# An attention of three stages ahead of two MLPs: four-head loads of q and k, and batch 0's normalisation moved between engines

## The chip, the cores and the metric

One core of a Trainium2 chip runs the whole program in one launch. The metric is the device time of an execution in microseconds (us), the median of several. The engines are TensorE (PE), VectorE (DVE), ScalarE (ACT), GpSimd (POOL) and the queues that issue DMAs, here those of SyncE (SP) and of ACT.

## The reference

```python
def _attn_ref(q, k, v):                 # B, H, S, D = 4, 8, 576, 64;  m = 32
    q_lm = q.reshape(B, H, m, S // m, D).mean(axis=3)      # 18 rows per landmark
    k_lm = k.reshape(B, H, m, S // m, D).mean(axis=3)
    A, Bm, C = sm(q, k_lm), sm(q_lm, k_lm), sm(q_lm, k)    # softmax of scale * a @ b.T
    Z = Bm.T / (norm1(Bm) * norminf(Bm) + 1e-6)
    for _ in range(6):
        Z = 2 * Z - Z @ Bm @ Z
    return A @ Z @ C @ v
def _moe_ref(x, w_gate, w_val, w_out, rms_g):              # 2304 x 512, d_ff = 1536
    xn = x / sqrt(mean(x * x) + 1e-6) * rms_g
    g = xn @ w_gate
    return (g * sigmoid(g) * (xn @ w_val)) @ w_out
def _moe2_ref(x, w_in, w_out, s, b):                       # 2304 x 512, d_ff = 2048
    r = maximum(x @ w_in, 0)
    return (s * r * r + b) @ w_out
```

The attention's output, heads side by side, is x of the first MLP, whose output is x of the second. The weights come as 64-bit floats.

## The kernel before

The program computes the attention batch by batch. For batch 0 it does so alone; the attention of batch b + 1 is laid under the first MLP's products of batch b. A batch has 12 units, one for each 128 columns of w_gate and w_val. A unit forms a small product of the two weight tiles with the attention's last factor (`gw`; the U product, L993, in `fused`), splits it into a high and a low part (`uh`, `ul`, L1001 to L1004), and then multiplies both with the high and low parts of A (`xh`, `xl`) in three products each (L1016, in `first_mm`), once for each half of the batch (hf). L1032 to L1038 form the hidden value from the results, and L1061 or L1065 multiply it with w_out. The second MLP follows (L975, L1091).

Attention, with its lines: q and k are loaded by `load_heads` (L446), for each of them in two groups g of four heads. A group fills a tile of 128 partitions, 32 for each head, each partition holding the 18 rows of one landmark. In batches 0 and 1 (`fine` is false) the heads of group g are 2h + g, so the load takes one DMA for each head. L474 sums the 18 rows (batch 0: on DVE; batch 1: by POOL, in the steps L488 to L493), L498 transposes the sums, L528 with L532 (ACT) transposes q and k themselves. L660 are scores: of C (`c_side`: maximum L677, Exp L687, transposed back L704 and evicted L714, times v in L726) and of A (`a_side`: transposed L756, maximum L757, subtracted L758, Exp L759, summed L762, scaled L767, transposed L768). L556 to L593 form Bm, L586 with L631 are the steps of the iteration for Z. L790 (DVE) opens the last part, the normalisation: L828 forms x, L834 (ACT) its squares, L848 sums them over columns, L855 to L859 make the root's reciprocal, L861 spreads it to a diagonal, L866 multiplies it out to all partitions, L872 scales A with it, and L876 (ACT) and L878 (POOL or DVE) split A into `xh` and `xl`. Only then can the batch's products run.

Weights of the first MLP are converted once, in batch 0 (`narrow`): a DMA (L906, L904) fills one of three `stage` tiles, ACT does L917 and L919, DVE L921 and L924. The result is also stored to DRAM (`kept`) and read back for the other batches.

The order of the work is made by a planner in the program (`Scheduler`). Each operation is given with the engines it may run on, an assumed duration on each, and a key; the planner plays the program with these durations and at each step gives an engine the ready operation with the smallest key. `S_.by_path` sets the keys of an attention batch by the longest path behind each operation. What the planner writes is fixed: each engine executes its own list in order. While PE would stand idle by the plan in the first 60 us of plan time, `warm` (L1248) puts filler products into its list, one for each 0.1 us.

## Time and profile before

| | us |
|---|---|
| median of 3 runs | 906.83 |
| lowest, highest | 901.38, 908.39 |
| the profiled execution, its own time | 903.9 |
| span of its instructions | 902.2 |
| PE busy in it | 870.2 (96%) |
| DVE busy | 700.9 (78%) |
| ACT busy | 430.0 (48%) |
| POOL busy | 114.4 (13%) |

The span runs from the first to the last instruction that the profiler has recorded. The mean granted clock of PE is 0.987 of full speed. Busy shares are means over stages of different kinds; the filler products count as busy too.

### The profile page before, as it was taken

How to read it: one execution, taken by the hardware profiler on the slowest of the kernel's cores; microseconds unless marked ns; L12 is line 12 of the kernel's file. 1: busy time of each engine (PE TensorE's matmuls, PEld its weight loads, DVE VectorE, ACT ScalarE, POOL GpSimd, SP SyncE). 2: the span in 40 equal slices, each digit the busy share in tenths (PEclk: the TensorE clock that was granted, in tenths of full speed). 3: DMA queues.
4: the chain of work that ended last, by engine and by line, in shares of the span. 5: the costliest groups of instructions: out<-in, count | busy, mean ns of one | idle time of the engine just before them, and what ended most of it. 6: DMA issues, size and time to landing. Idle time of an engine off the chain costs nothing.

```text
span 902.2 us, 17055 instructions
## 1 busy us (share of the span) xinstructions
PE 870.2 (96%) x6453; PEld 726.4 (81%) x6453; DVE 700.9 (78%) x1486; ACT 430.0 (48%) x902; POOL 114.4 (13%) x152
## 2 busy tenths in 40 slices
PE   8897899899999999999999999999999999999997
PEld 5576666798788898899888988888888888888896
DVE  5768889889888889799889866676667666666686
ACT  3565566535465345555656533343343334333453
POOL 0442034500465004300000000000000000000000
PEclk9898999999999999999999999999999999999999
DMA  7778998886444432348887200010001000100100
GB/s 162 198 214 283 247 280 236 271 241 216 119 144 141 143 116 84 106 146 272 286 262 252 56 1 1 0 47 1 1 1 47 1 1 1 47 1 1 27 22 24
DMA packets 72899, 105.99 MB, mean 117 GB/s; under 512 B 25968, under 2 KB 46448, under 8 KB 72816
## 3 DMA queue, kind: packets, MB, share of 16 engines
q1 hardware_dynamic: 72240, 103.45, 38.3%
q10 hardware_dynamic: 576, 1.44, 0.7%
q8 instruction: 51, 0.84, 0.4%
q14 instruction: 32, 0.26, 0.1%
HBM read 90.70 MB, written 14.16 MB: 116 GB/s over the span
## 4 chain that ended last, share of the span: by engine, by line
PE 83%; DVE 8%; DMA 5%; ACT 2%; issue 1%; SPq 1%; ACTq 0%; DVEq 0%
PE bank L975 22%; PE bank L1091 22%; PE bank L1016 15%; PE bank L1065 12%; PE bank L1061 3%; PE bank L993 3%; DMA region<-in_q_dram 2%; DVE cmag L921 2%; DMA stage<-in_moe_w_out_dram 2%; PE bank L648 1%; PE bank L828 1%; DMA stage<-in_moe_w_gate_dram 1%; PE bank L1248 1%; DVE wl L893 1%; DVE rawg L924 1%
## 5 line engine op out<-in xcount | busy, mean ns | idle before, releaser
L1016 PE MATMUL bank<-xh,uh 128*128 128x288 f32 x384 | 124.2, 323 | 6.4 <-DVE hbuf L1034 3.1
L975 PE MATMUL bank<-xh,ul 128*128 128x512 f32 (+1 forms) x320 | 117.7, 368 | 0.0
L975 PE MATMUL bank<-xh,uh 128*128 128x512 f32 (+1 forms) x320 | 117.6, 368 | 0.0
L975 PE MATMUL bank<-xl,uh 128*128 128x512 f32 (+1 forms) x320 | 117.6, 368 | 0.0
L1016 PE MATMUL bank<-xl,uh 128*128 128x288 f32 x384 | 114.8, 299 | 0.0
L1016 PE MATMUL bank<-xh,ul 128*128 128x288 f32 x384 | 114.7, 299 | 0.0
L1091 PE MATMUL bank<-wh,hh 128*128 128x512 f32 x288 | 112.4, 390 | 0.3 <-DVE hh L892 0.3
L1091 PE MATMUL bank<-wl,hh 128*128 128x512 f32 x288 | 112.3, 390 | 0.0
L1226 ACT ACTIVATE hbuf<-bank 128x512 f32<-128x512 f32 (+1 forms) x79 | 43.9, 556 | 143.4 <-PE bank L975 143.3
L1091 PE MATMUL bank<-wh,hl 128*128 128x512 f32 x288 | 112.0, 389 | 0.0
L1016 PEld LDWEIGHTS bank<-xh,uh 128*128 128x128 f32 x384 | 73.6, 192 | 27.3 <-issue 5.0
L1065 PE MATMUL bank<-hh,wh 128*128 128x288 f32 x288 | 87.9, 305 | 1.1 <-ACT xbuf L1075 1.1
L1065 PE MATMUL bank<-hl,wh 128*128 128x288 f32 x288 | 84.9, 295 | 0.1
L1065 PE MATMUL bank<-hh,wl 128*128 128x288 f32 x288 | 84.6, 294 | 0.0
L893 DVE TENSOR_TENSOR hl<-hbuf,hh 128x512 fp32r<-128x512 f32 (+2 forms) x123 | 73.1, 595 | 2.3
L1016 PEld LDWEIGHTS bank<-xl,uh 128*128 128x128 f32 x384 | 73.7, 192 | 0.5
L1016 PEld LDWEIGHTS bank<-xh,ul 128*128 128x128 f32 x384 | 73.7, 192 | 0.0
L975 PEld LDWEIGHTS bank<-xh,uh 128*128 128x128 f32 x320 | 60.2, 188 | 11.1
L975 PEld LDWEIGHTS bank<-xl,uh 128*128 128x128 f32 x320 | 60.0, 188 | 10.9
L975 PEld LDWEIGHTS bank<-xh,ul 128*128 128x128 f32 x320 | 60.1, 188 | 10.2
L917 ACT ACTIVATE ca<-stage 128x512 f32<-128x512 f32 x68 | 45.9, 675 | 42.6 <-DMA stage<-in_moe_w_out_dram 12.0
L892 DVE CAST uh<-region 128x512 fp32r<-128x512 f32 x56 | 23.9, 426 | 54.4 <-PE bank L975 54.4
(193 smaller groups left out, 1822.9 us busy)
## 6 DMA issues: line engine op xcount, KB each, us to landing
rawo<-kepto SPq DMA_DIRECT2D x84, 256.0 KB, 3.3
rawg<-keptg SPq DMA_DIRECT2D x36, 512.0 KB, 3.9
stage<-in_moe_w_out_dram SPq DMA_DIRECT2D x28, 512.0 KB, 5.2
stage<-in_moe_w_in_dram SPq DMA_DIRECT2D x16, 512.0 KB, 4.6
stage<-in_moe_w_gate_dram SPq DMA_DIRECT2D x12, 512.0 KB, 5.3
stage<-in_moe_w_val_dram SPq DMA_DIRECT2D x12, 512.0 KB, 5.5
keptg<-rawg SPq DMA_DIRECT2D x12, 512.0 KB, 6.3
region<-in_k_dram SPq DMA_DIRECT2D x32, 144.0 KB, 5.3
```

Source lines behind the costliest of these rows:

```text
L648: nc.tensor.matmul(out=ps.t[:, 0:HC], lhsT=part(u, "bd")[:, 128 * e:128 * e + 128], rhs=part(y, "t").rearrange("p (t e i) -> p t e i", e=2 ...
L892: else e.tensor_copy(out=hi(), in_=src())), r=r, w=[wh], pair=True)
L893: b = op({"dve": t_dve(n), "pool": t_pool(n)}, key, lambda e: e.tensor_tensor(out=lo(), in0=src(), in1=hi().bitcast(F32), op=ALU.subtract) ...
L917: op(("act", 0.08 + t_act(512)), key, lambda e: e.activation(out=a.t, in_=word(1).bitcast(F32), func=ACTF.Copy, scale=2.0 ** -112), r=[st, ...
L921: op(("dve", t_dve(512)), key, lambda e: e.scalar_tensor_tensor(out=m.t, in0=word(1), scalar=-2 ** 31, in1=m.t, op0=ALU.bitwise_and, op1=A ...
L975: nc.tensor.matmul(out=ps.t[:, 0:n], lhsT=w[a].t[:, ks], rhs=x[y].t[:, kd, 0:n], start=(kd == 0 and i == 0), stop=(kd == KD - 1 and i == 2))
L993: nc.tensor.matmul(out=pU[g].t[m, 0:256], lhsT=gw[b].t[p, m], rhs=r.t[p, :, 128 * k:128 * k + 128], start=True, stop=True)
L1016: nc.tensor.matmul(out=ps.t[:, 0:HC], lhsT=u[a].t[:, 256 * g + 128 * part:256 * g + 128 * part + 128], rhs=x[y].t.rearrange("p k n -> p (k ...
L1061: nc.tensor.matmul(out=A[c].t[:, 0:HC], lhsT=r.t[:, 128 * c:128 * c + 128], rhs=h.t, start=(f == 0), stop=(f == F1 - 1))
L1065: nc.tensor.matmul(out=A[c].t[:, 0:HC], lhsT=w[a].t[:, 128 * c:128 * c + 128], rhs=hs[y].t[:, 0:HC], start=(f == 0 and i == 0), stop=(f == ...
L1091: nc.tensor.matmul(out=A[c].t, lhsT=hs[a].t[:, s], rhs=w[y].t, start=(f == 0 and i == 0), stop=(f == F2 - 1 and i == 2))
L1226: e.activation(out=r.t[:, 0:n], in_=ps.t[:, 0:n], func=ACTF.Relu) if e is nc.scalar
```

## The change

In batches 0 and 1 group g now holds heads 4g to 4g + 3, which lie behind each other in DRAM, so one DMA loads all 128 partitions; q of batch 0 goes on SP's queue as well, and the planner's assumed duration of such a load is 3.64 in place of 5.2. What follows needs heads 2h + g, so scores, and the product for Bm, take each head from the tile that holds it (`loaded`), read both tiles, and both tiles of k (or q) are transposed ahead of the first of them. In batch 0 the four squares are added up on DVE before L848, which then has one product in place of four for each third (until now only the other batches did so); the diagonal (L861) and the low parts of A (L878) are given to DVE alone instead of to DVE or POOL. A Tanh on a dummy tile loads ACT's table behind the second root. The U product of batch 0's first unit has a smaller key. In every batch the diagonal, the adds and the low parts are marked as sharing the planner's port between DVE and POOL (`pair`).

```diff
@@ -417,6 +417,9 @@
         def dp(n):
             return {"dve": t_dve(n), "pool": t_pool(n)}
 
+        def near(n):
+            return {"dve": t_dve(n)} if first else dp(n)
+
         pair = xs[1, b] = (Buf(x_r[0]), Buf(x_r[1]))
         area = {"t": (0, SEG * D), "bd": (SEG * D, 256)}
 
@@ -442,13 +445,17 @@
                 t = src[nm, g] = Buf(qk_r[nm, g])
 
                 def load_heads(e, t=t, a=a, g=g):
+                    if not fine:
+                        e.dma_start(
+                            out=t.t.rearrange("p (t d) -> p t d", d=D),
+                            in_=a[b, 4 * g:4 * g + 4].rearrange("h (i t) d -> (h i) t d", t=SEG))
+                        return
                     for h in range(4):
                         e.dma_start(
                             out=t.t[32 * h:32 * h + 32].rearrange("p (t d) -> p t d", d=D),
                             in_=a[b, 2 * h + g].rearrange("(i t) d -> i t d", t=SEG))
 
-                at(("act" if first and nm == "q" else "sp", 2.2 if first and nm == "q" else 5.2),
-                   -0.3 if b else 0, load_heads, w=[t])
+                at(("sp", 5.2 if fine else 3.64), -0.3 if b else 0, load_heads, w=[t])
...
+        def loaded(g, h):
+            n = 2 * h + g
+            return n // 4, slice(32 * (n % 4), 32 * (n % 4) + 32)
 
         lmT, bd, tt = {}, {}, {}
...
@@ -552,10 +565,10 @@
             for g in range(2):
                 if not fine:
                     for h in range(4):
-                        p = slice(32 * h, 32 * h + 32)
+                        i, p = loaded(g, h)
                         nc.tensor.matmul(
-                            out=pB.t[p, 32 * g:32 * g + 32], lhsT=bd["q", g].t[0:D, p],
-                            rhs=bd["k", g].t[0:D, p], start=True, stop=True)
+                            out=pB.t[32 * h:32 * h + 32, 32 * g:32 * g + 32], lhsT=bd["q", i].t[0:D, p],
+                            rhs=bd["k", i].t[0:D, p], start=True, stop=True)
                     continue
                 for e in range(2):
                     nc.tensor.matmul(
@@ -640,7 +653,7 @@
                     else e.tensor_copy(out=zy(1), in_=v2(pY2))), r=[pY2], w=[ZY])
 
         def scores(ps, nm, g, hf, p0, r, w):
-            d, t = bd["kq"[nm == "k"], g], tt[nm, g]
+            other = "kq"[nm == "k"]
...
@@ -655,19 +668,21 @@
                 return
             def mm(_):
                 for h in range(4):
-                    p = slice(32 * h, 32 * h + 32)
+                    i, p = loaded(g, h)
                     e = slice(D * hf, D * hf + D)
                     nc.tensor.matmul(
-                        out=ps.t[p, 0:HC], lhsT=d.t[e, p],
-                        rhs=t.t[e].rearrange("p (t m) -> p t m", m=128)[:, :, p], start=True, stop=True)
-
-            at(("pe", SCORE), p0 + 0.02, mm, r=[d, *[(t, i) for i in range(3)], *r], w=[ps, *w])
+                        out=ps.t[32 * h:32 * h + 32, 0:HC], lhsT=bd[other, i].t[e, p],
+                        rhs=tt[nm, i].t[e].rearrange("p (t m) -> p t m", m=128)[:, :, p], start=True, stop=True)
+
+            at(("pe", SCORE), p0 + 0.02, mm, r=[*[bd[other, j] for j in range(2)],
+                *[(tt[nm, j], i) for j in range(2) for i in range(3)], *r], w=[ps, *w])
 
 
         Cv = Buf(cv_r)
 
         def c_side(g, p0):
-            transposed("k", g, p0)
+            for j in (g,) if fine else (0, 1) if g == 0 else ():
+                transposed("k", j, p0)
...
@@ -739,7 +754,8 @@
 
         def a_side(hf, g, p0):
             if hf == 0:
-                transposed("q", g, p0)
+                for j in (g,) if fine else (0, 1) if g == 0 else ():
+                    transposed("q", j, p0)
...
@@ -834,13 +850,12 @@
                 at(("act", t_act(HC)), p0 + 0.01, lambda e, c=c, pX=pX, xq=xq: e.activation(
                     out=xq.t[:, HC * c:HC * c + HC], in_=pX.t[:, 0:HC], func=ACTF.Square), r=[pX], w=[(xq, c)])
             pS, pR, rs, dg = Buf(ps_r), Buf(ps_r), Buf(sm_r), Buf(a_ring)
-            if not first:
-                for c, n in ((2, 2 * HC), (1, HC)):
-                    at(dp(n), p0 + 0.03, lambda e, c=c, n=n, xq=xq: e.tensor_tensor(
-                        out=xq.t[:, 0:n], in0=xq.t[:, 0:n], in1=xq.t[:, HC * c:HC * c + n], op=ALU.add),
-                        r=[(xq, i) for i in range(KD)] if n > HC else [(xq, 0), (xq, c)],
-                        w=[(xq, 0)] + ([(xq, 1)] if n > HC else []))
-            n_sum = KD if first else 1
+            for c, n in ((2, 2 * HC), (1, HC)):
+                at(near(n), p0 + 0.03, lambda e, c=c, n=n, xq=xq: e.tensor_tensor(
+                    out=xq.t[:, 0:n], in0=xq.t[:, 0:n], in1=xq.t[:, HC * c:HC * c + n], op=ALU.add),
+                    r=[(xq, i) for i in range(KD)] if n > HC else [(xq, 0), (xq, c)],
+                    w=[(xq, 0)] + ([(xq, 1)] if n > HC else []), pair=True)
+            n_sum = 1
 
...
@@ -857,12 +872,15 @@
 
             at(("dve", 0.3), p0 + 0.06, s_rec, r=[pS], w=[rs])
             at(("act", 0.2 if first else 1.4), p0 + 0.07, lambda e, rs=rs: e.activation(
-                out=rs.t[0:NP, 0:3], in_=rs.t[0:NP, 0:3], func=ACTF.Sqrt), r=[rs, "table"], w=[rs])
-            at(dp(HC), p0 + 0.07, lambda e, rs=rs, dg=dg: e.tensor_tensor(
+                out=rs.t[0:NP, 0:3], in_=rs.t[0:NP, 0:3], func=ACTF.Sqrt), r=[rs, "table"], w=[rs, ("root", b, hf)])
+            if first and hf:
+                at(("act", 1.4), 0.0, lambda e: e.activation(out=spare, in_=spare, func=ACTF.Tanh),
+                   r=[("root", 0, 0), ("root", 0, 1)], w=["spare"])
+            at(near(HC), p0 + 0.07, lambda e, rs=rs, dg=dg: e.tensor_tensor(
                 out=dg.t[0:NP].rearrange("p (j c) -> p j c", j=3),
                 in0=ident[0:NP, 0:NP].unsqueeze(1).to_broadcast([NP, 3, NP]),
                 in1=rs.t[0:NP, 0:3].rearrange("p (j o) -> p j o", o=1).to_broadcast([NP, 3, NP]),
-                op=ALU.mult), r=[rs, "ident"], w=[dg])
+                op=ALU.mult), r=[rs, "ident"], w=[dg], pair=True)
...
@@ -875,9 +893,9 @@
                 at({"act": t_act(HC), "dve": t_dve2(HC)}, p0 + 0.09, lambda e, a=a, cols=cols: (
                     e.activation(out=part(0, "t")[:, cols], in_=a.t[:, 0:HC], func=ACTF.Copy) if e is nc.scalar
                     else e.tensor_copy(out=part(0, "t")[:, cols], in_=a.t[:, 0:HC])), r=[a], w=wh, pair=True)
-                at(dp(HC), p0 + 0.1, lambda e, a=a, cols=cols: e.tensor_tensor(
+                at(near(HC), p0 + 0.1, lambda e, a=a, cols=cols: e.tensor_tensor(
                     out=part(1, "t")[:, cols], in0=a.t[:, 0:HC], in1=part(0, "t")[:, cols].bitcast(F32),
-                    op=ALU.subtract), r=[a, wh[0]], w=wl)
+                    op=ALU.subtract), r=[a, wh[0]], w=wl, pair=True)
...
@@ -994,7 +1012,7 @@
                         out=pU[g].t[m, 0:256], lhsT=gw[b].t[p, m],
                         rhs=r.t[p, :, 128 * k:128 * k + 128], start=True, stop=True)
 
-        op(("pe", U_PE), key, mm, r=[gw[b], (r, 0), (r, 1)], w=[*pU, (uh, "taken"), (ul, "taken")])
+        op(("pe", U_PE), key - 12 if not (b or f) else key, mm, r=[gw[b], (r, 0), (r, 1)], w=[*pU, (uh, "taken"), (ul, "taken")])
         for g in range(2):
             c = slice(256 * g, 256 * g + 256)
             op({"act": t_act(256), "dve": t_dve(256)}, key, lambda e, g=g, c=c: (
```

The lists that the planner makes of it differ on all engines. In the new program's lines, L449 is the four-head load, L924 the load of a weight part (L906 before), L955 the store L937.

SP's queue from its beginning, before; `stage` tiles are those of the weights:

```order
L446 DMA region<-in_k_dram 32x1152 x8
L460 DMA region<-in_v_dram 32x8x64 x18
L906 DMA stage_91<-in_moe_w_gate_dram 128x4x128
L446 DMA region<-in_k_dram 32x1152 x8
L446 DMA region<-in_q_dram 32x1152 x8
L906 DMA stage_91<-in_moe_w_val_dram 128x4x128
L937 DMA keptg_114<-rawg_85 128x1024
L460 DMA region<-in_v_dram 32x8x64 x18
L906 DMA stage_91<-in_moe_w_gate_dram 128x4x128
```

and now:

```order
L449 DMA region<-in_k_dram 128x1152 x2
L449 DMA region<-in_q_dram 128x1152 x2
L467 DMA region<-in_v_dram 32x8x64 x18
L924 DMA stage_91<-in_moe_w_gate_dram 128x4x128
L449 DMA region<-in_k_dram 128x1152 x2
L449 DMA region<-in_q_dram 128x1152 x2
L467 DMA region<-in_v_dram 32x8x64 x18
L924 DMA stage_91<-in_moe_w_val_dram 128x4x128
L955 DMA keptg_114<-rawg_85 128x1024
L454 DMA region<-in_k_dram 32x1152 x4
L924 DMA stage_91<-in_moe_w_gate_dram 128x4x128
```

(Of each run of three stage loads the first is shown; three small loads stand behind the first run in both.) The second group of v, batch 1's, now stands ahead of the fourth to sixth stage loads instead of behind them, and half of batch 2's k ahead of the seventh.

DVE's list in the last part of batch 0's attention, from L790 on, before (three pieces: its start, the parts of the fourth weight, the scaling of A):

```order
L790 TENSOR_TENSOR region<-bank_63,mask_74 128x128 x2
L798 TENSOR_TENSOR region<-region,mask_75 128x256
L855 TENSOR_SCALAR region<-bank_65 96x3
L810 TENSOR_TENSOR gw_106<-bank_64,gT 128x128
L921 SCALAR_TENSOR_TENSOR cmag_97<-stage_91,cmag_97 128x512
L924 SCALAR_TENSOR_TENSOR rawg_86<-ca_95,cmag_97 128x512
L872 TENSOR_TENSOR region<-region,bank_66 128x288 x2
L872 TENSOR_TENSOR region<-region,bank_63 128x288 x2
L1034 SCALAR_TENSOR_TENSOR hbuf<-hbuf,bank_70 128x288
```

and now, where L854 are the adds of squares, L879 the diagonal, L890 the scaling, L896 the low parts, L939 and L942 the weight conversion:

```order
L806 TENSOR_TENSOR region<-bank_67,mask_74 128x128 x2
L814 TENSOR_TENSOR region<-region,mask_75 128x256
L854 TENSOR_TENSOR region<-region 128x576
L854 TENSOR_TENSOR region<-region 128x288
L870 TENSOR_SCALAR region<-bank_68 96x3
L879 TENSOR_TENSOR xbuf<-ident,region 96x288
L890 TENSOR_TENSOR region<-region,bank_63 128x288 x2
L896 TENSOR_TENSOR xl_83<-region,xh_81 128x288 x2
L895 CAST xh_81<-region 128x288
L939 SCALAR_TENSOR_TENSOR cmag_97<-stage_91,cmag_97 128x512
L942 SCALAR_TENSOR_TENSOR rawg_86<-ca_95,cmag_97 128x512
L896 TENSOR_TENSOR xl_83<-region,xh_81 128x288 x2
```

The conversion of the fourth to sixth weight part has moved from between the normalisation's steps to behind the first low parts, and steps that POOL did stand in DVE's list.

PE's list where batch 1's attention ends and its first unit begins, before (L866 is the scaling product, L993 with `gw1` the U product of batch 1's first unit, L1061 products with w_out):

```order
L1061 MATMUL bank0_63<-hbuf_108,rawo2_90 128x288
L866 MATMUL bank6_69<-region_113,ones_72 128x288 x2
L993 MATMUL bank5_68<-rawg2_87,gw0_106 32x256
L1016 MATMUL bank4_67<-xh0_81,uh0_98 128x288
L1061 MATMUL bank2_65<-hbuf_108,rawo0_88 128x288
L1061 MATMUL bank2_65<-hbuf_108,rawo1_89 128x288
L993 MATMUL bank4_67<-rawg0_85,gw1_107 32x256
```

and now (L1011 is the U product, L884 the scaling product, L1079 the product with w_out, L1034 with `xh1` batch 1's first product):

```order
L1011 MATMUL bank6_69<-rawg0_85,gw1_107 32x256
L1079 MATMUL bank2_65<-hbuf_108,rawo0_88 128x288
L863 MATMUL bank7_70<-ones_72,region_113 96x1 x3
L1079 MATMUL bank1_64<-hbuf_108,rawo1_89 128x288
L884 MATMUL bank7_70<-region_113,ones_72 128x288
L884 MATMUL bank6_69<-region_113,ones_72 128x288
L1079 MATMUL bank0_63<-hbuf_108,rawo2_90 128x288
L1034 MATMUL bank4_67<-xh1_82,uh0_98 128x288
```

(Rows between are left out.) The scaling products of batch 1 now stand behind the U product of its first unit and close ahead of its first product; before they stood one unit further ahead.

## Rows read from the trace of the kernel before

**Rows 1.** Table of stretches: busy us (instructions) of each engine, clock, DMA share, GB/s

```profile
0.00:61.00 61.00, 52.44 (x627) 38.06 (x628) 38.57 (x110) 29.56 (x75) 14.64 (x24) 0.89 0.76 181
61.00:175.00 114.00, 100.49 (x967) 74.62 (x966) 99.52 (x225) 69.84 (x152) 40.20 (x52) 0.96 0.88 268
175.00:484.00 309.00, 303.73 (x2894) 265.69 (x2892) 269.97 (x622) 161.62 (x375) 59.56 (x77) 1.00 0.57 179
```

**Rows 2.** Timeline, first 30 us: start, duration, engine, line, what; in brackets idle before

```profile
0.80 8.41 ACTq L446 DMA_DIRECT2D region<-in_q_dram  x8
0.80 8.12 SPq L446 DMA_DIRECT2D region<-in_k_dram  x8
...
8.71 2.12 DVE L474 TENSOR_REDUCE region<-region 128x64 f32<-128x1152 f32 x1 [7.13 <-DMA region<-in_k_dram]
...
13.62 6.30 DVE L474 TENSOR_REDUCE region<-region 128x64 f32<-128x1152 f32 x3 [2.78 <-DMA region<-in_k_dram]
```

**Rows 3.** DMA rates in 40 slices: 2.5 to 13.5 (q, k), then 24.5 to 28 (weights first)

```profile
GB/s 369 369 268 201 184 235 201 184 201 218 268 268 201 184 201 218 184 201 201 218 268 268 201 184 201 218 201 184 201 218 268 268 201 184 201 218 141 139 174 203
DMA packets 1278, 2.40 MB, mean 218 GB/s; under 512 B 786, under 2 KB 786, under 8 KB 1278
...
GB/s 398 374 386 374 374 375 375 339 363 363 363 351 386 363 351 363 351 363 363 386 374 328 271 225 168 98 127 167 207 101 206 206 258 182 223 54 265 159 317 212
```

**Rows 4.** Timeline, 20 to 33 us: the first weight tile and who waits

```profile
20.64 0.45 SPq L906 DMA_DIRECT2D stage<-in_moe_w_gate_dram  x1
...
25.15 0.66 ACT L917 ACTIVATE ca<-stage 128x512 f32<-128x512 f32 x1 [2.57 <-DMA stage<-in_moe_w_gate_dram]
...
26.68 1.53 PE L726 MATMUL bank<-region 128*32 128x64 f32 x40 [2.20 <-ACT region L714]
...
32.03 1.21 PE L726 MATMUL bank<-region 128*32 128x64 f32 x40
...
32.23 0.29 DVE L631 SCALAR_TENSOR_TENSOR region<-region,bank 128x128 f32<-128x128 f32 x1 [4.33 <-issue]
```

**Rows 5.** Timeline, 43 to 61 us: the normalisation of batch 0 up to the first product

```profile
43.25 0.47 DVE L790 TENSOR_TENSOR region<-bank,mask 128x128 f32<-128x128 f32 x2
...
45.72 4.26 PE L848 MATMUL bank<-ones,xbuf 128*96 128x1 f32 x48
...
52.84 4.16 PE L1248 MATMUL bank<-ones 128*128 128x256 bf16 x35
...
58.53 1.54 POOL L878 TENSOR_TENSOR xl<-region,xh 128x288 fp32r<-128x288 f32 x2 [7.10 <-ACT xh L876]
...
59.45 1.58 PE L1248 MATMUL bank<-ones 128*128 128x256 bf16 x13
...
60.79 0.38 PE L1016 MATMUL bank<-xh,uh 128*128 128x288 f32 x1
```

**Rows 6.** Groups by line and form, first 80 us: busy us, mean ns, idle before

```profile
L872 DVE TENSOR_TENSOR region<-region,bank 128x288 f32<-128x288 f32 x4 | 1.6, 451 | 2.4 <-PE bank L866 2.4
```

**Rows 7.** Timeline, POOL and DVE: one instruction beside POOL's, and without

```profile
39.37 1.41 POOL L488 TENSOR_TENSOR region<-region 128x576 f32<-128x576 f32 x1
39.98 1.35 DVE L921 SCALAR_TENSOR_TENSOR cmag<-stage,cmag 128x512 int32<-128x512 int32 x1
...
76.91 0.68 DVE L921 SCALAR_TENSOR_TENSOR cmag<-stage,cmag 128x512 int32<-128x512 int32 x1
```

**Rows 8.** SP's queue: its waits up to 175 us (total, times, longest), then timeline

```profile
SPq L906 <- DVE cmag L921: 33.8, 14, 5.7
...
47.64 11.07 SPq L460 DMA_DIRECT2D region<-in_v_dram  x18
58.81 0.40 SPq L906 DMA_DIRECT2D stage<-in_moe_w_gate_dram  x1
```

**Rows 9.** Timeline: first hidden value of batch 0, last L866 and first product of batch 1

```profile
62.70 0.46 DVE L1034 SCALAR_TENSOR_TENSOR hbuf<-hbuf,bank 128x288 f32<-128x288 f32 x1 [2.23 <-ACT hbuf L1032]
...
161.00 0.72 PE L866 MATMUL bank<-region,ones 96*128 96x288 f32 x2 [2.69 <-DVE region L872]
...
175.07 0.51 PE L1016 MATMUL bank<-xh,uh 128*128 128x288 f32 x1
```

## The prediction

> **What bounds the kernel now.** I read the table of stretches first, then the timeline of the start, then the waits. From 175 us on, TensorE (PE) is busy 303.7 of 309 us at full clock, and this change leaves the order of PE's work the same from the sixteenth U product (L993) on, so that part can only be shifted, not shortened [rows 1]. What can shrink lies before. Up to 61 us the core computes batch 0's attention, on which every product waits; PE shows 52 busy us there, but much of it is filler. From 61 to 175 us nothing is full: PE 100.5 of 114 us, VectorE (DVE) 99.5, DMA engines at 0.88 [rows 1].
>
> In the start the reader is to see three things. First, k and q come in as 32-partition pieces, eight issues on each of two queues; the first segment sum starts at 8.71 us, the other three wait until 13.62 and end at 19.92 [rows 2]. Second, DVE stands still for 4.33 us before the first step of the inverse (L631): ScalarE (ACT) has waited 2.57 us for the first weight tile with the evictions queued behind it, PE's next group then waited for those evictions, and L631 for PE [rows 4]. Third, from the L790 that opens the last part (43.25 us) to the first product (L1016, 60.79) is 17.5 us, in which PE runs 63 filler products in three groups (35, 15 and 13) [rows 5]; its queue is in order, so real work stands behind them.
>
> **The sum** is made against the profiled execution, 903.9 us (span 902.2 and 1.7 around it), which is 2.9 under the median of the three runs.
>
> *Loads.* Sixteen 144 KB issues become four of 576 KB, all on SP; the ACT queue is freed of eight issues. In 32-partition form the engines were occupied throughout and moved 218 GB/s, while 128-partition weight tiles ran at some 365 GB/s [rows 3]. A 512 KB tile landed 4.5 us after its issue (20.64 to 25.15) [rows 4]; so I put k's first tile at 0.8 + 4.5 + 0.2 = 5.5 us and the next three 1.6 us apart (590 KB at 365 GB/s): 7.1, 8.7, 10.3. The four sums take 2.1 us each on DVE (6.30 / 3) [rows 2] and then run back to back, 5.5 to 13.9 instead of to 19.9: **−6.0**. Bounds: if the rate stays at 218 GB/s (2.7 us each, first at 6.6) they end at 16.8, −3.1; if only the bytes counted, the first landed at 2.4 and they ended at 10.8, −9. I take the weight tiles' rate since the new transfers have their 128 partitions.
> A rule of the Trainium skill speaks against this: "DMA: Bandwidth & Descriptors", in the section on why a DMA increments its semaphore by 16, says that a transfer is split over the largest number up to 16 that divides its slowest dimension, so 32 and 128 partitions both use 16 engines and the new form would have no more of them than the old. By that alone this term would be the −3.1 and the sum 897; the two rates in rows 3 say otherwise, and I follow them.
>
> *The wait for the first weight tile.* SP issues 18 loads of v and then the weight tiles; with four k and q issues in place of eight ahead of them (8.12 us for eight [rows 2]) they move up by some 4 us, and ACT has its twelve evictions and the moved Exp work to do before it asks for the tile. **−2.6**, ACT's wait; bounds 0 (it finds another wait) and −4.3 (DVE's whole gap).
>
> *From L790 to the first product.* Removed: PE's 24 column sums become 6 (48 records, 4.26 us [rows 5]), and the filler falls from 161 products to 110 in all. Moved from GpSimd (POOL) to DVE: the scale's diagonal (2), the low parts (4, of which POOL's first two took 1.54 us [rows 5]). Added on DVE: four adds of squares, two of 576 and two of 288 columns. The new order puts 26 DVE instructions between L790 and the first product: 5 of 512 or 576 columns at about 0.7 us [rows 7], 14 of 256 or 288 at 0.45 [rows 6], 7 small ones at 0.2 (0.47 for L790's two [rows 5]): 3.5 + 6.3 + 1.4 = 11.2 us, on one engine, so DVE and no longer PE sets this part. But POOL now runs batch 1's four segment sums at the same time, and a DVE instruction with two SBUF inputs took 1.35 us beside POOL's L488 and 0.68 without [rows 7]. Eleven of the 26 are of that kind; at 0.25 each that adds 2.8: 14.0 in place of 17.5, **−3.5**. Bounds: no meeting, 11.2, −6.3; every one held by 0.67, 18.6, +1.1. I take a value nearer the low end since POOL's later, short steps hold less than L488.
> The skill's "SBUF — State Buffer" (section on the single rule) says that the port pair is an exclusive lock and the later of the two engines stops for the other's whole instruction. By it the high bound would be the usual case where POOL comes first; L921's pair of durations agrees that one can lose that much.
>
> *What is given back.* Before, DVE had converted six weight parts by the first product; in the new order three. The other three, 1.36 us each (two instructions of 0.68 [rows 7]), 4.1 us, now stand behind it, where DVE had 2.23 us idle before the first L1034 [rows 9]: **+1.9**, bounds 0 and +4.1. The one Tanh on a dummy moves its 1.28 us table load from behind the first product to before it, beside DVE work; covered, unless ACT is late with the high parts, then +1.3. The first U product (L993) issued earlier: nothing, since in the old order too it stands ahead of the three filler groups.
>
> *Between 61 and 175 us* weights stream through three stage tiles: SP's loads wait 33.8 us in total for DVE's L921 to free one [rows 8]. This chain started late: v of batch 1, 11.07 us of issues, stood ahead of the seventh load at 58.81. Now v goes out before the fourth load: it waits for batch 0's last L726 (32.03 before [rows 4], some 8 us earlier now), so its issues end near 36, in time for the fourth L921 near 48; and the seventh load waits for the fourth L921, which stands one instruction behind the first low parts, about 49: 10 us earlier, the same as the sum. So I carry it through.
>
> Sum: −6.0 − 2.6 − 3.5 + 1.9 = −10.2: **894 us**.
>
> **Rivals.**
> (a) *The start is shorter, the weight stream isn't.* For: DVE gets 5 us of new work (four adds 2.4, two diagonals 0.9, four low parts 1.8) and is at 99.5 of 114 us in the stretch that follows. Against: DVE idles over 22 us of the first 61 [rows 1]. Taking away the 5 us and the 1.9 from the load and ACT terms alone: −8.6 + 6.9 = −1.7, **902 us**.
> (b) *POOL holds DVE through the whole last part*: +1.1 in place of −3.5, **899**. For: POOL's sums now fill the stretch from the inverse on. Against: before, only some of the meetings cost the full 0.67.
> (c) *Loads no faster*: −3.1 in place of −6.0, **897**.
> (d) *Slower: batch 1's hand-over.* Both k tiles are now transposed before its first scores and both q tiles before its first A, and its last scaling products (L866) stand after the thirteenth U, seven L1061 ahead of the first use of their result, while before they ended at 161.0 and were first used at 175.1 [rows 9]: 14 us of slack are gone. If batch 1 does not come forward with the start, PE waits there. It costs nothing up to an end at 173; for a loss of 1% it must end at 185, 24 us later than now, and the time is then **917**. Against: two more table loads (2.6 us) and a second set of transposes are all that is added to it.
>
> **Chances.** A measurement of this kernel can tell about 1%, 9 us, from no change. Forecast 0.52 (888 to 897); (a) 0.19; (b) 0.10; (c) 0.12; (d) 0.07. The range takes all of the bounds at the low end (−9 − 4.3 − 6.3 = −19.6, 884) and (a) at the high, with something for the median lying above the profiled run: 884 to 905. Against the median of 906.8, faster by over 1% means under 897.8: the forecast and most of (c): 0.61; within 1%: (a), (b), the rest of (c): 0.31; slower: (d) and a little for waits I have not seen: 0.08.
>
> **What would show it.** Loads: the first segment sum near 5.5 us and the fourth ending near 14; at 17 the rate did not rise. Wait: no gap of over 2 us on ACT at the first L917. Last part: first product (L1016) near 48.7 us; DVE nearly full before it. Stream: seventh weight load near 49, batch 1's first product near 165 instead of 175. It is wrong if batch 0's first product comes early and batch 1's does not: then (a), or (d) if PE waits at L866 or the product behind it.

## The result, and the profile after

| kernel | median us | lowest to highest | profiled run: span, clock |
|---|---|---|---|
| before | 905.40 | 901.38 to 908.39 (4 runs) | 902.2, 0.987 |
| changed | 894.64 | 892.64 to 895.60 (4 runs) | 890.9, 0.994 |

The ratio is 0.9877 (95% interval 0.9848 to 0.9906): 10.8 us faster. The prediction was 894. Four later runs of the changed kernel gave 894.88, ratio 0.9880 (0.9850 to 0.9909). So the total was right; the sections below show that two of the sum's four terms were too small and two too large, and that these errors cancel.

In the changed kernel the lines are numbered anew: L449 loads k and q (L446 before), L487 sums segments (L474), L644 is the inverse's step (L631), L806 opens the last part (L790), L1034 is a product (L1016), L924 loads a stage tile (L906), L935, L939 and L942 convert it (L917, L921, L924), L1011 is a U product (L993).

The table of stretches after, the columns as in [rows 1]:

```profile
0.00:61.00 61.00, 49.04 (x625) 35.37 (x625) 51.36 (x134) 35.88 (x87) 22.02 (x33) 0.97 0.80 232
61.00:175.00 114.00, 102.33 (x977) 75.98 (x978) 98.15 (x231) 68.47 (x151) 31.69 (x41) 0.97 0.83 259
175.00:484.00 309.00, 304.39 (x2867) 266.83 (x2866) 271.69 (x627) 166.97 (x380) 57.08 (x73) 1.00 0.57 181
```

VectorE gained 12.8 busy us in the first 61 us, since work that used to lie later fits in there, and some of it is held up; from 175 us on nothing changed. The timeline of the start and of the first steps after it, which answers to [rows 2, 4, 8]:

```profile
0.80 0.88 SPq L449 DMA_DIRECT2D region<-in_k_dram  x2
1.73 0.90 SPq L449 DMA_DIRECT2D region<-in_q_dram  x2
2.67 13.09 SPq L467 DMA_DIRECT2D region<-in_v_dram  x18
4.75 8.32 DVE L487 TENSOR_REDUCE region<-region 128x64 f32<-128x1152 f32 x4 [3.17 <-DMA region<-in_k_dram]
15.80 0.45 SPq L924 DMA_DIRECT2D stage<-in_moe_w_gate_dram  x1
20.37 0.67 ACT L935 ACTIVATE ca<-stage 128x512 f32<-128x512 f32 x1 [0.77 <-DMA stage<-in_moe_w_gate_dram]
21.81 0.29 DVE L644 SCALAR_TENSOR_TENSOR region<-region,bank 128x128 f32<-128x128 f32 x1 [0.24 <-PE bank L599]
...
49.71 0.38 SPq L924 DMA_DIRECT2D stage<-in_moe_w_gate_dram  x1
```

The four sums run back to back and end at 13.07 instead of 19.92. ScalarE waits 0.77 instead of 2.57 us for the first weight tile, and L644 comes 10.4 us before the old L631. The seventh stage load goes out at 49.71 instead of 58.81. The last part, against [rows 5, 7]:

```profile
34.27 0.49 DVE L806 TENSOR_TENSOR region<-bank,mask 128x128 f32<-128x128 f32 x2 [0.19 <-PE bank L599]
...
35.83 2.65 POOL L504 TENSOR_TENSOR region<-region 128x256 f32<-128x256 f32 x3
38.68 2.45 DVE L854 TENSOR_TENSOR region<-region 128x576 f32<-128x576 f32 x2
39.01 1.80 POOL L501 TENSOR_TENSOR region<-region 128x576 f32<-128x576 f32 x1
...
47.99 0.81 DVE L896 TENSOR_TENSOR xl<-region,xh 128x288 fp32r<-128x288 f32 x2
48.44 2.23 PE L1266 MATMUL bank<-ones 128*128 128x256 bf16 x19 [0.90 <-ACT region L545]
50.43 0.38 PE L1034 MATMUL bank<-xh,uh 128*128 128x288 f32 x1
```

A pair of adds of squares, one of 576 and one of 288 columns, takes 2.45 us beside GpSimd's sums. The low parts are ready at 48.8, but 19 filler products stand ahead of the first product in TensorE's queue, and these had waited 0.90 us for ScalarE's L545, an eviction for batch 1. The part is 16.16 us long, against 17.54 before.

### The profile page after: what moved, and what is told of

It is laid out like the page before. It is cut to its first block, busy times and chain, and to the rows that moved or that the text cites. A ratio compares the mean times of both kernels' runs of the same rounds, so it can differ in the third digit from the quotient of the medians.

```text
span 890.9 us, 16830 instructions
## 1 busy us (share of the span) xinstructions
PE 858.0 (96%) x6366; PEld 716.2 (80%) x6366; DVE 703.2 (79%) x1500; ACT 431.7 (48%) x900; POOL 110.8 (12%) x147
## 4 chain that ended last, share of the span: by engine, by line
PE 80%; DVE 8%; DMA 5%; ACT 3%; issue 2%; SPq 1%; DVEq 0%; ACTq 0%
PE bank L993 22%; PE bank L1109 22%; PE bank L1034 13%; PE bank L1083 12%; PE bank L1079 3%; PE bank L1011 2%; DMA stage<-in_moe_w_val_dram 2%; DVE cmag L939 1%; PE bank L661 1%; DMA region<-in_v_dram 1%; DMA stage<-in_moe_w_gate_dram 1%; DVE wl L911 1%; ACT ca L935 1%; PE bank L844 1%; PE bank L599 1%
## 5 line engine op out<-in xcount | busy, mean ns | idle before, releaser
L1034 PE MATMUL bank<-xh,uh 128*128 128x288 f32 x384 | 123.5, 321 | 6.7 <-DVE hbuf L1052 2.6
L993 PE MATMUL bank<-xh,ul 128*128 128x512 f32 (+1 forms) x320 | 117.7, 368 | 0.0
L993 PE MATMUL bank<-xl,uh 128*128 128x512 f32 (+1 forms) x320 | 117.6, 368 | 0.0
L993 PE MATMUL bank<-xh,uh 128*128 128x512 f32 (+1 forms) x320 | 117.6, 367 | 0.0
L1034 PE MATMUL bank<-xl,uh 128*128 128x288 f32 x384 | 114.2, 297 | 0.0
L1034 PE MATMUL bank<-xh,ul 128*128 128x288 f32 x384 | 114.0, 297 | 0.0
L1034 PEld LDWEIGHTS bank<-xh,uh 128*128 128x128 f32 x384 | 73.0, 190 | 27.2 <-issue 4.2
L1034 PEld LDWEIGHTS bank<-xl,uh 128*128 128x128 f32 x384 | 73.2, 191 | 0.6
L1034 PEld LDWEIGHTS bank<-xh,ul 128*128 128x128 f32 x384 | 73.2, 191 | 0.0
L993 PEld LDWEIGHTS bank<-xh,uh 128*128 128x128 f32 x320 | 60.2, 188 | 11.3
L993 PEld LDWEIGHTS bank<-xl,uh 128*128 128x128 f32 x320 | 60.0, 188 | 10.9
L993 PEld LDWEIGHTS bank<-xh,ul 128*128 128x128 f32 x320 | 60.1, 188 | 10.1
L935 ACT ACTIVATE ca<-stage 128x512 f32<-128x512 f32 x68 | 45.8, 673 | 42.1 <-DMA stage<-in_moe_w_out_dram 10.9
```

Source lines behind the costliest of these rows:

```text
L935: op(("act", 0.08 + t_act(512)), key, lambda e: e.activation(out=a.t, in_=word(1).bitcast(F32), func=ACTF.Copy, scale=2.0 ** -112), r=[st, ...
L993: nc.tensor.matmul(out=ps.t[:, 0:n], lhsT=w[a].t[:, ks], rhs=x[y].t[:, kd, 0:n], start=(kd == 0 and i == 0), stop=(kd == KD - 1 and i == 2))
L1034: nc.tensor.matmul(out=ps.t[:, 0:HC], lhsT=u[a].t[:, 256 * g + 128 * part:256 * g + 128 * part + 128], rhs=x[y].t.rearrange("p k n -> p (k ...
```

## The experiments

All runs in one table. Two instants carry the argument: the first product, and the last U product, after which every kernel's profile runs another 429 to 432 us to its end. Both are of the one profiled execution, which can lie some us off the median: 900.5 us in pieces, 897.7 in loads_only, 926.1 in wide_fine, 894.0 in stage4.

| kernel | median us | ratio to before (interval) | first product | last U product |
|---|---|---|---|---|
| before | | 1 | 60.79 | 471.2 |
| changed | 894.64 | 0.9877 (0.9848 to 0.9906) | 50.43 | 461.0 |
| after_again | 894.88 | 0.9880 (0.9850 to 0.9909) | 51.97 | 463.2 |
| pieces | 905.08 | 0.9979 (0.9943 to 1.0015) | 58.75 | 468.3 |
| loads_only | 894.82 | 0.9858 (0.9807 to 0.9909) | 50.40 | 466.0 |
| loads_again | 895.38 | 0.9878 (0.9853 to 0.9902) | 51.77 | 463.9 |
| no_loads | 903.25 | 0.9969 (0.9947 to 0.9991) | 63.63 | 470.7 |
| few_sums | 891.84 | 0.9843 (0.9802 to 0.9885) | 47.30 | 456.4 |
| less_warm | 897.89, one run | | 47.94 | 466.4 |
| empty_tanh | 894.18, one run | | 51.14 | 462.9 |
| pe_sums | 905.13 | 0.9987 (0.9970 to 1.0005) | 65.77 | 472.3 |
| wide_fine | 920.52 | 1.0163 (1.0119 to 1.0207) | 59.68 | 493.1 |
| stage4 | 891.08 | 0.9838 (0.9772 to 0.9903) | 57.64 | 462.5 |
| stage4v | 889.22 | 0.9809 (0.9769 to 0.9849) | 53.73 | 456.6 |

### Which part carries the gain

**pieces**, the changed kernel with only batch 0's load form undone:

```diff
-  e.dma_start(out=t.t..., in_=a[b, 4 * g:4 * g + 4].rearrange("h (i t) d -> (h i) t d", t=SEG))
+  for h in range(4):          # k on SP, q on the ACT queue
+      e_.dma_start(out=...t[32 * h:32 * h + 32]..., in_=a_[b, 4 * g_ + h]...)
```

> The changed kernel in its own order on TensorE, VectorE, GpSimd and (but for the issues) ScalarE; only batch 0's k and q come in again as 32-partition pieces, eight issues on SP and eight on the ACT queue, as in the kernel before. Theory: the loads' form gave 6.85 us at the segment sums and most of the next 3.6 us at the wait for the first weight tile. Then the first segment sum starts at 8 to 9 us, the fourth ends at 19 to 20, ScalarE waits for the first weight tile again, the first product comes at 58 to 61 us instead of 50.4, and the time is 901 to 905. Rival: the other edits (squares added, low parts on VectorE) carry the gain and the loads are hidden: first product under 54 us, time under 898.

The rates from 3 to 9 us, which answer to [rows 3]: the table of stretches once more, its last two columns the share of the DMA engines' time and GB/s. Before:

```profile
3.00:9.00 6.00, 3.39 (x20) 2.40 (x18) 0.29 (x1) 0.00 (x0) 0.00 (x0) 0.99 1.04 216
```

The changed kernel:

```profile
3.00:9.00 6.00, 5.85 (x36) 4.38 (x33) 4.25 (x3) 2.83 (x7) 0.00 (x0) 1.00 1.04 384
```

Pieces:

```profile
3.00:9.00 6.00, 2.32 (x12) 1.49 (x10) 0.41 (x1) 0.00 (x0) 0.00 (x0) 1.00 1.04 219
```

In both forms the engines are full; the bytes per second are not the same. The sums, the first weight tile and the inverse's step in pieces:

```profile
8.59 2.12 DVE L498 TENSOR_REDUCE region<-region 128x64 f32<-128x1152 f32 x1 [7.01 <-DMA region<-in_k_dram]
13.39 6.28 DVE L498 TENSOR_REDUCE region<-region 128x64 f32<-128x1152 f32 x3 [2.68 <-DMA region<-in_k_dram]
27.17 0.68 ACT L946 ACTIVATE ca<-stage 128x512 f32<-128x512 f32 x1
29.50 0.29 DVE L655 SCALAR_TENSOR_TENSOR region<-region,bank 128x128 f32<-128x128 f32 x1 [0.25 <-PE bank L610]
```

The sums start at 8.59 and end at 19.67, and the first product comes 8.3 us later, 6.6 of it at the sums: on the time the theory holds (the median lies at the edge of its range), and rival (c) of the prediction falls. On the wait for the first weight tile it missed: in this order ScalarE stands idle for nothing ahead of L946, though the loads are the slow ones. From the last sum to the inverse's step are 9.8 us, against 12.3 before and 8.7 in the changed kernel, so the loads account for 1.1 us of that step. The other 2.5 came with the new order, or with TensorE's clock, which was 0.57 from 25 to 33 us before and 1.00 from 20 to 29.5 in pieces; no run tells these two apart.

**loads_only** is the kernel before plus the loads (the mark `pair` stays on the diagonal and the low parts); **loads_again** is the same kernel again; **no_loads** is the rest without the loads.

```diff
  loads_only:  - return {"dve": t_dve(n)} if first else dp(n)    + return dp(n)
               - n_sum = 1                                       + n_sum = KD if first else 1
               - Tanh on spare; - key - 12 for the first U product
  no_loads:    the same lines put into the kernel before
```

> The kernel before with the four-head loads of batches 0 and 1 (and the pairing of heads that they bring) and nothing else: 24 column sums on TensorE, diagonal and low parts where the planner puts them, no added Tanh. Theory: the loads carry about 10 of the 11 us up to the last part, which is then as long as before (17.5 us from the step that opens it to the first product): first product at 51 to 53 us, time 894 to 898. Rival: without the shorter last part the early start is lost in it: first product at 56 us or later, time 900 or more.

> The kernel with only the four-head loads once more, for a narrower interval. Theory: the rest of the change brings nothing in this order, the median lies within 1.5 us of the changed kernel's 894.6. Rival, from the kernel without the loads (3 us faster than before): the rest brings 2 to 3 us and this median is 896.5 to 898.

> The kernel before with all of the change but its loads: squares added on VectorE, diagonal and low parts there, one Tanh. Theory by the trace of the changed kernel: its last part is 1.4 us shorter than before, so the first product is at 58 to 61 us and the time 902 to 906, no difference that can be told. Rival, the prediction's sum: the last part is 3.5 us shorter wherever it starts, first product at 57 to 58 us, time 899 to 902.

With the loads alone the time is that of the whole change, in eight runs. Its last part, in two profiles, is no longer than the changed kernel's, with 24 column sums on TensorE and the low parts on GpSimd (L894; L877 is the diagonal). The table of stretches, from the step that opens the last part to the first product, of loads_only, loads_again, changed, after_again and no_loads; the granted clock is the column before the last two:

```profile
34.48:50.40 15.92, 15.60 (x125) 11.07 (x124) 9.44 (x23) 10.49 (x25) 8.32 (x11) 0.79 0.58 171
34.72:51.77 17.05, 15.89 (x126) 12.47 (x125) 9.09 (x23) 9.92 (x25) 7.64 (x10) 0.80 0.56 159
34.27:50.43 16.16, 12.46 (x111) 9.13 (x110) 15.02 (x30) 10.97 (x28) 11.97 (x15) 1.00 0.72 207
34.68:51.97 17.29, 12.55 (x102) 8.86 (x101) 16.49 (x33) 10.97 (x28) 12.48 (x17) 0.92 0.70 199
42.98:63.63 20.65, 17.52 (x122) 12.93 (x122) 18.76 (x34) 11.45 (x28) 14.34 (x17) 0.75 0.75 205
```

The clock differs even between two executions of one program, and no run holds it fixed. GpSimd's timeline in loads_only:

```profile
39.95 0.66 POOL L877 TENSOR_TENSOR xbuf<-ident,region 96x288 f32<-96x288 f32 x1 [5.93 <-ACT region L875]
...
43.00 1.41 POOL L501 TENSOR_TENSOR region<-region 128x576 f32<-128x576 f32 x1
44.51 1.56 POOL L894 TENSOR_TENSOR xl<-region,xh 128x288 fp32r<-128x288 f32 x2
```

It stands waiting for 5.93 us with real steps at the head of its queue, and three of batch 1's four sums (L501) begin at 43.00 or later, so VectorE meets little. My theory had expected 17.5; it was right on the time, and on the part wrong by 1.6 us in one profile and 0.5 in the other. Without the loads the rest gives 2.8 us (0.8 to 4.8), although its last part is 20.65 us long: the planner put 49 fillers ahead of the first product, as TensorE's timeline has them, and the clock was 0.56 from 47.5 to 57.5 us:

```profile
57.75 6.12 PE L1253 MATMUL bank<-ones 128*128 128x256 bf16 x49
63.63 0.38 PE L1021 MATMUL bank<-xh,uh 128*128 128x288 f32 x1
```

The theory's range held on the time, but the difference can be told, which it had denied, and it missed on the first product (58 to 61 expected). The parts do not add: the rest is worth 1 to 5 us alone, and beside the loads nothing that the intervals (some 2.5 us to either side) let see. The earlier key of the first U product moves nothing: without it the program comes out the same, instruction for instruction.

### The last part: GpSimd, filler, Tanh

**few_sums** shortens batch 1's sums on GpSimd, all else in the same order (it adds only four of the 18 rows, so its output isn't the reference's):

```diff
-  e.tensor_tensor(out=y(), in0=x()[:, 0:9], in1=x()[:, 9:18], op=ALU.add)    # then 4, 2, 1
+  e.tensor_tensor(out=y()[:, 0:2], in0=x()[:, 0:2], in1=x()[:, 9:11], op=ALU.add)
```

> The changed kernel in the same order, but batch 1's segment sums on GpSimd leave out most of their work: of 18 rows only four are added, in two short instructions instead of five, so GpSimd works some 2 us instead of 16 between 30 and 47.5 us. Theory: GpSimd holds VectorE's two-input instructions there; without it those between 34 and 48 us fall from 0.8 to 1.6 us to 0.68 to 0.8, about 3 us in all, and the first product moves from 50.4 to 47.0 to 48.5; time 891 to 893.5. Rival: VectorE doesn't set this part (filler on TensorE and waits on ScalarE do): first product within 0.5 us of 50.4, time within 1 us of the changed kernel's.

Its VectorE timeline, against the 2.45 above:

```profile
35.96 1.24 DVE L856 TENSOR_TENSOR region<-region 128x576 f32<-128x576 f32 x2
37.12 0.75 DVE L856 TENSOR_TENSOR xbuf<-xbuf 128x576 f32<-128x576 f32 x1
```

The same pair of adds takes half the time; the add of 288 columns alone fell from 1.54 to 0.46 us. The first product is at 47.30, the last part 13.99 us long. The clock was 1.00 in this part, as in the changed kernel's profile. The theory holds on the part: the meeting costs it 2.2 us. The median is 2.8 lower, which the two intervals don't separate.

**pe_sums** moves these sums to TensorE in full, with one copy behind each:

```diff
+  for n in range(SEG):
+      nc.tensor.matmul(out=pM.t[:, 0:D], lhsT=ident, rhs=s3.t[:, D * n:D * n + D], start=(n == 0), stop=(n == SEG - 1))
```

> The changed kernel with batch 1's segment sums on TensorE: 18 matmuls per tile with the identity as weights, accumulated in one bank, and one copy, in place of five GpSimd instructions; nothing is left out. Theory: GpSimd no longer meets VectorE between 30 and 47.5 us, the same 3 us as with the short sums, and the 72 matmuls of 0.12 us lie where filler ran: first product at 47 to 49 us, time 891 to 894. Rival: TensorE's queue is in order and four groups of 2.2 us stand ahead of real work: first product at 50 us or later, time 894 to 898.

TensorE's timeline:

```profile
42.32 4.23 PE L503 MATMUL bank<-region,ident 128*128 128x64 f32 x36
...
56.11 5.88 PE L1278 MATMUL bank<-ones 128*128 128x256 bf16 x29 [2.81 <-ACT region L508]
61.83 4.13 PE L503 MATMUL bank<-region,ident 128*128 128x64 f32 x36
65.77 0.38 PE L1046 MATMUL bank<-xh,uh 128*128 128x288 f32 x1
```

VectorE's adds were as short as in few_sums (1.25), but a group of 18 took 4.13 to 4.23 us, twice what I had put in, and the last group and 29 fillers stood ahead of the first product. The clock was at its 1.2 GHz level, 0.50, from 55 to 60 us, so these fillers ran slow as well. The rival's mechanism holds; the loss is larger than it had said (894 to 898), and the whole gain is gone.

**less_warm** leaves out the 19 fillers, **empty_tanh** the Tanh:

```diff
  less_warm:   + if 87 <= n_warm[0] <= 105: return
  empty_tanh:  - lambda e: e.activation(out=spare, in_=spare, func=ACTF.Tanh)   + lambda e: None
```

> The changed kernel in the same order without the 19 filler products that stand on TensorE ahead of the first product. Theory: the first product's inputs are ready at 48.8 us and the filler (48.44 to 50.4) is all that holds it, so it starts at 48.8 to 49.1, and the products behind it follow; the 14th U product, 165.8 us now, comes at 164 to 165, the time is 891 to 894. Rival: VectorE, which has the next weight parts to make, holds what follows, and the 14th U product stays within 0.4 us of 165.8; if the clock falls without the filler, the granted clock of 48 to 61 us shows it and the products there take twice as long.

> The changed kernel in the same order without the Tanh on the dummy tile. Theory: its table load (45.13, 1.28 us) lies beside VectorE's work and costs nothing, nor does it bring much: first product within 0.4 us of 50.4, the first Tanh of a product at 52.6 to 53.0 instead of 51.5, the 14th U product within 0.6 us of 165.8, time 892 to 896. Rival: the load holds the high parts that follow it on ScalarE (0.8 us), and the first product comes 0.5 to 1 us earlier without it.

In less_warm the first matmul starts at 47.94 and the second, which reads the low parts, at 48.95 instead of 50.65, as the theory said. But the fourth U product is at 65.25, before that 65.06: the lead is gone, and the 14th comes at 170.77, 5.0 us later, where neither the theory nor the rival had it. Two stretches in the table, of the changed kernel:

```profile
50.00:60.00 10.00, 7.84 (x82) 6.61 (x80) 8.95 (x19) 6.10 (x13) 0.00 (x0) 1.00 0.79 239
120.00:140.00 20.00, 19.88 (x217) 13.50 (x217) 18.51 (x49) 11.18 (x26) 13.28 (x16) 1.00 0.88 237
```

And of less_warm:

```profile
50.00:60.00 10.00, 6.55 (x62) 5.42 (x60) 8.38 (x18) 6.38 (x14) 0.00 (x0) 0.83 0.77 230
120.00:140.00 20.00, 17.97 (x188) 11.37 (x178) 14.76 (x37) 7.86 (x19) 9.26 (x12) 0.74 0.87 243
```

The granted clock (the column before the last two) was lower in both: 0.83 right behind the missing filler, and 0.74 later, from 130 to 140 us about half (0.51), the 1.2 GHz level. So what took the lead away, VectorE or the clock, isn't separated. Whether the missing filler made the clock fall, one run can't tell: in after_again, with the filler, it fell too, to 0.72 from 50 to 55 us. Empty_tanh missed its bounds by little: first product 51.14, 14th U product 167.67; but after_again, with the Tanh, has 51.97 and 167.02, and in empty_tanh the 19 fillers took 3.75 us instead of 2.23, at a clock of 0.50 from 47.5 to 50 us. The table load now stands at 49.63, again ahead of the product that needs it, and the first Tanh follows the product's start by 1.07 us here and in the changed kernel. The Tanh costs and brings nothing that shows.

### What sets the stretch behind it

**wide_fine** gives batches 2 and 3 one transfer per tile too, with every other head:

```diff
-  for h in range(4):
-      e.dma_start(out=t.t[32 * h:32 * h + 32]..., in_=a[b, 2 * h + g]...)
+  e.dma_start(out=t.t, in_=a[b].rearrange("(h g) (i t) d -> g h i (t d)", g=2, t=SEG)[g])
```

> The changed kernel, its order on the compute engines kept, with k and q of batches 2 and 3 also loaded as one 128-partition transfer of 576 KB per tile instead of four 32-partition ones (the heads of a tile stay every other one). Theory: what gave the 6.85 us at the start is the rate of the form; between 40 and 128 us batch 2's four tiles run beside the weight stream, and at 360 instead of 218 GB/s they free 4 us of the transfers' time and 5 us of SP's issues. ScalarE's waits for stage tiles shrink, the 14th U product comes at 162 to 165 us instead of 165.8, time 890 to 893.5. Rival: between 61 and 175 us VectorE sets the pace, not the transfers; 14th U product within 0.5 us of 165.8, time 893.5 to 896.

> The changed kernel once more, beside the run above: 893 to 896 us, and the loads-only kernel (895.4 in eight runs) no more than 2 us above it if the rest of the change brings next to nothing; 892 or less if the rest brings 3 us.

It is 25.6 us slower than after_again. SP issued one such tile at 44.52 and nothing else until 57.08. The stretch from 48 to 53 us:

```profile
48.00:53.00 5.00, 4.77 (x32) 2.88 (x30) 2.17 (x7) 2.99 (x7) 1.47 (x4) 0.50 0.25 98
```

A quarter of the DMA engines' time and 98 GB/s: my theory, "128 partitions give the rate", was wrong in this form. The Trainium skill, "DMA: Bandwidth & Descriptors", in the section on why a DMA increments its semaphore by 16, says that a transfer is split over the largest number up to 16 that divides the slowest dimension of both sides. This source's is 4 heads, and a share of 0.25 agrees with 4 of 16. That accounts for slow tiles of batch 2 and 3, though how much of the 25.6 us is theirs no run separates; it does not account for the first product's delay to 59.68, of which 4.3 us were there at the step that opens the last part, before the first such load (44.52). The granted clock of the first 61 us was 0.75 against 0.94 in after_again, and why is open.

**stage4** adds a fourth stage tile, **stage4v** that and fewer, longer runs for v:

```diff
+  stage4 = Slot(far[:, 3, 0:1024].bitcast(I64)); st_r.slots.append(stage4)     # xbuf columns, freed after batch 0
   stage4v also:
-  for n in range(SEG): e.dma_start(out=vt()[32 * (n % 4):..., n // 4], in_=sv[token(b, n)])
+  for n in range(8): e.dma_start(out=vp()[32 * (n % 4):..., :, 2 * D * (n // 4):...], in_=two[:, :, 2 * D * n:2 * D * n + 2 * D])
```

> The changed kernel with a fourth stage tile for the weight stream, put into columns of the output buffer that nothing uses between batch 0's attention and batch 2's outputs; its order is the planner's for four tiles. Theory: from the first product to 165 us the round trip of three stage tiles (5.3 us to land, then ScalarE's and VectorE's steps) keeps the stream late, and with four ScalarE's waits for stage tiles (some 8 us in the changed kernel between 61 and 175 us) go: U products 8 to 13 come 2 to 6 us earlier, time 888 to 892.5. Rival: VectorE (98 of 114 us) or the transfers (0.83) set that stretch: time 893 to 897, waits moved to another engine.

> As the run above, and v of batches 0 and 1 in 10 issues with 512-byte runs instead of 18 with 256-byte runs (the columns of the transposed C are grouped so that tokens next to each other fall into one partition). Theory: SP's 13.1 us of v issues at the start become 7 to 8, the first weight load is issued near 10 instead of 15.8, ScalarE no longer waits for its tile, and the three loads that stand behind batch 1's v come 4 us earlier; 0.5 to 2 us below the run above. Rival: the time of v lies in its runs' bytes and its issues are hidden: within 0.5 us of the run above.

In both, one tile of the second layer's input weights waits in the fourth slot until 393 us while batch 2's outputs are written over it at 383.6, so that tile isn't the reference's; the instructions are the same. ScalarE's waits for stage tiles from 61 to 175 us (total, times, longest), in the changed kernel:

```profile
ACT ca L935 <- DMA stage<-in_moe_w_val_dram: 4.8, 4, 1.6
ACT ca L935 <- DMA stage<-in_moe_w_out_dram: 2.8, 3, 1.5
ACT ca L935 <- DMA stage<-in_moe_w_gate_dram: 1.3, 2, 1.1
```

In stage4:

```profile
ACT wh L912 <- DMA rawo<-kepto: 3.8, 3, 2.7
ACT ca L938 <- DMA xbuf<-in_moe_w_gate_dram: 1.6, 1, 1.6
ACT ca L938 <- DMA xbuf<-in_moe_w_val_dram: 0.5, 1, 0.5
```

The 8.9 us for stage tiles became 2.1, but 3.8 us of waits for stored weights read back came in their place. Stage4's first product came 7.2 us later than the changed kernel's, with the clock at 0.50 from 42.5 to 57.5 us, and its last U product 1.5 us later: the stream caught up. It did not where the theory had it: the U products 8 to 13 came 6 to 10 us later, not 2 to 6 earlier, and counted from the first product they lie between 1.3 us earlier and 3.3 later; by that count it is ahead only from the 14th on (3.6 us). So that the shorter waits for stage tiles are the gain isn't shown. Stage4v issued its first weight load at 11.49 instead of 15.21, and comes out 1.9 us lower, which the intervals don't separate. Its interval hardly touches those of the changed kernel, so this points to a faster version; one that gives the slot back in time wasn't tried.

## Why the prediction was right, point by point

| step | predicted | measured | second profile (after_again) |
|---|---|---|---|
| loads, end of the segment sums | -6.0 | -6.85 | -6.99 |
| wait for the first weight tile (to L644) | -2.6 | -3.57 | -1.9 |
| L644 to L806, not in the sum | 0 | +1.44 | +0.3 |
| L806 to the first product | -3.5 | -1.38 | -0.25 |
| give-back (first product to last U) | +1.9 | +0.2 | +0.8 |
| last U product | -10.2 | -10.2 | -8.0 |

- *Loads, right.* The rate is the form's, 384 against 216 GB/s; the first sum at 4.75 was forecast for 5.5. Which part of the form sets it, partitions, bytes per transfer or the number of queues, wasn't separated; wide_fine shows that 128 partitions and 576 KB alone are not enough.
- *The wait, right in size, in its mechanism only in part.* ScalarE's wait fell by 1.8 us. But pieces has none there with the slow loads, and after_again has none either while L644 waits for TensorE:

```profile
19.34 0.65 ACT L935 ACTIVATE ca<-stage 128x512 f32<-128x512 f32 x1
23.34 0.29 DVE L644 SCALAR_TENSOR_TENSOR region<-region,bank 128x128 f32<-128x128 f32 x1 [1.91 <-PE bank L599]
```

TensorE's clock was 0.71 from 17.5 to 23.3 us there. In four profiles with this order and a clock of 1.00 up to this step (changed, few_sums, less_warm, empty_tanh) it comes 8.7 to 8.8 us behind the last sum, in after_again 10.4. The sum has no term for the clock; the profile before had 0.57 from 25 to 33 us, the changed one 1.00 up to L644, so part of the -3.57 is probably the clock's; how much, no run shows. The next row's +1.44 goes the other way: the clock was 0.66 from 30 to 35 us in the changed kernel's profile and 1.00 in after_again's, where the row is +0.3.

- *From L790 to the first product, wrong.* VectorE's own path was sized well: the low parts are ready 14.5 us behind L806 (14.0 put in), and the price of meeting GpSimd was near the estimate (2.8 put in, 2.2 found by few_sums). What the sum left out is filler: 19 products, 2.23 us at full clock, in a queue in order. After_again had them at 3.61 us, where the clock was 0.72 from 50 to 55 us. Above all, the step counted on a part that would be 17.5 us long without these edits; with the loads alone it is 15.92 and 17.05 (loads_only, loads_again), with the edits too 16.16 and 17.29. So the edits brought this part nothing that shows. The loads' kernels had the lower clock there (0.79 and 0.80 against 1.00 and 0.92), so what the edits do at an equal clock is open.
- *Give-back, too high.* One of the three conversions that it put behind the first product ran ahead of it, from 48.99 to 50.41 us, under the filler; why the others cost nothing is open. This miss (1.7) and that of the step above (2.1) nearly cancel, as do the smaller ones of the first three rows; that the last row agrees to a tenth is luck, and the second profile has -8.0. The prediction gave the rest of the change -1.6 together; the loads' kernels and the changed one put it near 0.
- *Carried through 61 to 175 us, right here*: the seventh load at 49.71 (49 forecast), batch 1's first product at 163.90 (165). It is no law: against the kernel before no_loads is 2.8 us late at the first product and 0.5 early at the last U; against the changed kernel stage4 is 7.2 late and 1.5 late.
- *Rivals.* (a) didn't come: batch 1's first product moved with the start, and VectorE stayed at 98 of 114 us. (b) came in part, as L854 beside L504 and L501 shows (its terms add up to 898.3, not 899). (d) didn't: against [rows 9], the last L884 ended at 162.8 and the product behind it began at 163.90.

## What to carry to other kernels

A load that arrives in thin slices is worth one wide transfer where everything waits for it, but look at the outermost dimension of both sides: with four heads in front a wide one fell below half the slices' rate. Moving work from GpSimd to VectorE brought nothing here, where what GpSimd did instead met VectorE at the same place; undo each half alone before crediting either. Filler on an in-order queue is work on the path wherever real work stands behind it, at nearly twice the price when the clock is low. Read the clock of a stretch before crediting its length to an edit.

## What the runs showed of the hardware

- An add of 576 and one of 288 columns on VectorE, both inputs in SBUF: 1.24 us together with GpSimd idle, 2.45 beside its sums; the one of 288 columns 0.46 and 1.54.
- A 128-partition transfer whose source's outermost dimension is 4: 98 GB/s at a DMA share of 0.25; 384 GB/s at full share where heads and rows merge; 32-partition pieces fill the engines at 216 to 219. Why full engines move so little there wasn't tried.
- 19 fillers: 2.23 us at a clock of 1.00, 4.21 in stage4 at the lower level, in the same program place (the second line; the first is after_again's, between the two):

```profile
48.71 3.61 PE L1266 MATMUL bank<-ones 128*128 128x256 bf16 x19 [0.98 <-ACT region L545]
53.78 4.21 PE L1274 MATMUL bank<-ones 128*128 128x256 bf16 x19 [0.76 <-ACT region L548]
```

- TensorE's clock differs between two executions of one program: 1.00 and 0.71 from 17.5 to 23.3 us, 1.00 and 0.72 from 50 to 55 us (changed, after_again). What makes it fall wasn't tried.
- 18 fp32 matmuls with 64 moving columns and 128 x 128 weights show as 36 records and take 4.13 to 4.23 us.
